# A chain of attention and two feed-forward layers on one core: a broadcast reciprocal row and a shared value product in the first batch

## The chip, the cores and the metric

One core of a Trainium2 chip runs the whole program. The metric is the device time of one execution in microseconds (us). The engines are TensorE (PE for its matmuls, PEld for its weight loads), VectorE (DVE), ScalarE (ACT), GpSimd (POOL) and SyncE (SP), which here only issues DMAs.

## What is computed

The inputs are q, k, v of shape (4, 8, 576, 64) and a decay f of shape (4, 8, 576). The reference, cut to what matters:

```
scores = q k^T / 8 + cum[i] - cum[j]        # cum: running sum of log(clip(f)), causal
attn   = exp(scores - max) / (sum + 1e-9)
x      = attn v                             # then heads side by side: 2304 tokens x 512
h      = x w_in;   g = max(h,0) + alpha*min(h,0);   x = g w_out      # layer 1, 512 -> 2048 -> 512
h      = x w2_in;  g = 0 | (h+1)^2/4 | h;           out = g w2_out   # layer 2
```

The weights of the two layers come as 64-bit floating point.

## The kernel before

The program is written as tasks (`add`: engine, estimated duration, position, dependencies), and `Order.emit` places them into one fixed order per engine, with estimated durations and latencies. An engine then runs its list strictly in that order: an instruction that waits holds up all that stand behind it. Only the order comes from the estimates.

Three kinds of work are laid over one another. The attention runs by units: each of the four batches is cut into a unit of 256 queries and one of 320, and a unit works through four pairs of heads. The conversion (`convert`, 32 pieces of layer 1's weights, w_in and w_out in turn) loads 512 KB, does two passes on ScalarE (L1170, L1203) and five on VectorE (L1173, L1182, L1190, L1195, L1209). Layer 1 (`l1_slice`) goes by chunks of 256 tokens and 16 slices: 12 matmuls L1257, the activation (L1267, L1270, L1276, L1279) and 12 matmuls L1296. The conversion of the first pieces and the first batch's attention start together; later batches and layer 1 share TensorE up to some 550 us, and layer 2 follows.

The first batch (units 0 and 1) takes another way than the later ones, and only it is touched (`plain_pair`). For a pair it loads k, q and v by SP (`load_tok`, L457 and L462), transposes k and q (L558, L576; copies L564, L584), and then goes by groups of two tiles of 64 queries, two heads beside one another on the 128 partitions. Per tile: scores (L622, L624, L627), the minimum on VectorE (`low`, L637), the exponential on ScalarE with the row sum (`expo`, L656), which is in `st`. Per group: the reciprocal of the sums (`rec`, L679 and L680), the multiplication of the whole probabilities by it (`scale`, L686, one VectorE instruction per tile, as wide as the keys: 320 to 576 in unit 1), transposes on TensorE (L704), copies to SBUF (L709), and the value product (L717). In unit 1 there are five tiles, so the third group has one tile alone. A value product has the keys in blocks of 128 and two matmuls to a block, one per head; the stationary operand is a window of `vF` that holds one head's values beside 64 columns of zeros, so both heads add into one PSUM tile `ps_o`. For the lone tile that is 5 blocks, 10 matmuls of 64 columns; each fp32 matmul stands as two records in the trace. At the pair's end ScalarE casts `ps_o` to the high part of x (`xhi`, L739) and VectorE makes the low part (`xlo`, L742).

In the later units the normalisation is another: unnormalised output, the sums gathered, inverted, written to DRAM (L1093) and read back as a broadcast row (L1097), and one VectorE multiplication (L1107).

At the start VectorE clears the rows past the sequence's end in its buffers: L449 for k, L451 for the two q buffers (`qr` for even pairs, three blocks from column 256 on; `qr1` for odd pairs). SP's list begins with f, the first k, q, v, three pieces of weights, alpha (2048 single words) and the second pair's q.

Of the kernel before, what the change touches and what calls it, by code (L numbers as in the profile page):

```python
# [9 lines left out]
F32 = mybir.dt.float32  # L10
# [181 lines left out]
def kernel(  # L192
# [98 lines left out]
    def add(eng, dur, fn, pos, *a, **k):  # L291
# [14 lines left out]
        raw=2, qr=1, qr1=1, q=2, k=2, S=7, M=3, r=2, PH=1, PL=1, s=3, o=1, h=2, g=4, gg=LH + 1,  # L306
        sums=2, rec=2, qd0=1, qd1=1, pA=4, pB=3, pt=4, st=3, sw=2, pty=2, raw2=NRAW, val2=NVAL, x2r=1,
# [84 lines left out]
    def open_phase(n):  # L392
        if n == 1:
            ph["x"] = la.enter_context(ExitStack())
            ph["p"] = ph["x"].enter_context(tc.tile_pool(name="ph1", bufs=1))
            ph["qr"] = ph["p"].tile([P, 3, 2, D], F32, name="qr1")
            names = ("vF",)
# [4 lines left out]
        for nm in names:  # L402
            cnt = NKB if n == 1 else 2 if nm == "vF" else NKB - 2
# [3 lines left out]
            (nc.vector if n == 1 else nc.gpsimd).memset(tf[:, :, 1, :], 0.0 if n == 1 or nm == "vL" else 1.0)  # L407
            if nm == "vF" and S % P:
                for x in (0, 2):
                    (nc.vector if n == 1 else nc.gpsimd).memset(t[S % P:, cnt - 1, x, :], 0.0)  # L410
# [39 lines left out]
    for t in (QR[0], ph["qr"]):  # L450
        nc.vector.memset(t[S % P:, 1:], 0.0)  # L451
# [55 lines left out]
    plain_pv = []  # L507
    attn_tasks = []
# [17 lines left out]
    plain_qk = [[], []]  # L526
    plain_tr = []

    def plain_pair(u, pr, pos_of, prev_pv):
# [12 lines left out]
        def load_q():  # L542
            qb.t = ph["qr"] if pr % 2 else QR[0].rearrange("p c j x d -> p (c j x d)")[:, :3 * P].rearrange(
                "p (c j d) -> p c j d", j=2, d=D)
# [33 lines left out]
        a = last["qtr"] = add("PE", 112 * np_, qtr, p0 - 1, [lq, last.get("qtr")], new=[pb], use=[qb])  # L578
        qready = []
# [10 lines left out]
        def choose():  # L590
# [5 lines left out]
        lv = add("SP", tok_issue(0, nk), lambda: load_tok(V["vF"][:, :, 0:3:2, :], v, b, pr, 0, nk), p0, prev_pv,  # L596
                 move=moved(2 * nk, 256))
# [7 lines left out]
        pvs = []  # L605
        st_new = [st]
        for g in range(-(-nt // 2)):
            tiles = [t for t in (2 * g, 2 * g + 1) if t < nt]
            pg = pos_of(2 * pr + 4 * g / nt)
            ps, sums_ = [], []  # L610
            for t in tiles:
# [57 lines left out]
                pd = []  # L669
                if nkey % P:  # L670
# [3 lines left out]
                    pd = [add("POOL", 150, pad, pg, ex, use=[pbuf])]  # L674
# [7 lines left out]
            rc = add("DVE", 140, rec, pg, sums_, use=[st])  # L682
            pready = []
            for t, (pbuf, nkey, pd) in zip(tiles, ps):
# [4 lines left out]
                pready += [add("DVE", dve2(nkey, True), scale, pg, [rc], use=[pbuf, st])] + pd  # L689
            nb_ = -(-(i0 + tiles[-1] + 1) // 2)  # L690
            per = 4 // len(tiles)
            for kb0 in range(0, nb_, per):
# [18 lines left out]
                def pv(tt=tt, kbs=kbs, nl=nl, w=w, g=g, nb_=nb_, first_=not pvs):  # L711
                    if first_:
                        ob.t = ps_a.tile([P, 512], F32, tag="o0", name="ps_o")
                    tv = tt.t[:, :w].rearrange("p (c t j q) -> p c t j q", t=nl, j=2, q=D)
                    for x, kb_ in enumerate(kbs):
                        for j in range(2):
                            nc.tensor.matmul(  # L717
                                out=ob.t[:, g * P:g * P + nl * D],
                                lhsT=V["vF"][:, kb_].rearrange("p a d -> p (a d)")[:, j * D:j * D + P],
# [7 lines left out]
                a = last["ppv"] = add("PE", 2 * len(kbs) * pe4(P), pv, pg, [a, lv, last.get("ppv")], new=[] if pvs else [ob],  # L727
# [3 lines left out]
        pn = pos_of(2 * pr + 1)  # L731
        t_ = b * S + q0
        o = 0
        while o < n:
# [3 lines left out]
            def xhi(c=c, x0=x0, o=o, m=m):  # L738
                nc.scalar.copy(out=xt(c)[pr][0][:, x0:x0 + m], in_=ob.t[:, o:o + m])  # L739

            def xlo(c=c, x0=x0, o=o, m=m):
                nc.vector.tensor_tensor(out=xt(c)[pr][1][:, x0:x0 + m], in0=ob.t[:, o:o + m],  # L742
                                        in1=xt(c)[pr][0][:, x0:x0 + m].bitcast(F32), op=ALU.subtract)

            a = add("ACT", act(m), xhi, pn, pvs + [("x", c)], use=[ob])
            l = add("DVE", dve(m), xlo, pn, [a], use=[ob])
            X_ready.setdefault(c, []).extend([a, l])
            attn_tasks.extend([a, l])
            o += m
        return pvs  # L750

    for u, pr in head_list():
# [18 lines left out]
        if u == 2 and pr == 0:  # L771
            phase2 = add("X", 0, lambda: open_phase(2), -50, plain_pv + [a for x in plain_qk for a in x])
# [1183 lines left out]
```

## Time and profile before

| what | value |
|---|---|
| median of 3 runs | 1033.4 us (1033.15 to 1033.97) |
| profiled execution, own time | 1034.34 us |
| its span in the trace | 1032.2 us |
| busy PE | 1009.0 us, 98% |
| busy DVE | 793.2 us, 77% |
| busy ACT | 647.5 us, 63% |
| chain that ended last | PE 67%, DVE 20%, ACT 6%, issue 4% |

The share of busy time is a mean over stages; a change to the first 135 us is read from that stretch. A busy TensorE can hide a small wait, since the ends of its matmuls are modelled. The profiled execution's time is 0.94 us over the median.

### The profile page before, as it was taken

To read this page: it belongs to the slowest core of one execution; us is meant where nothing else is said; L and a number is where in the kernel's file an instruction comes from. 1 tells how busy PE (TensorE), PEld (TensorE's weight loads), DVE (VectorE), ACT (ScalarE), POOL (GpSimd) and SP (SyncE) were. 2 spreads that over 40 slices of the span, in tenths; PEclk is the share of its full clock that TensorE was granted. 3 is DMA by queue.
4 is the path that set the end of the run, shared out by engine and by line. 5 is a ranking of instruction groups with operands and counts; after the bars stand their busy time and mean duration, and the time that the engine had idled before them with its cause. 6 is when DMAs were issued, how large, how long until landed. Compare 5 with 4: busy or idle time off the path is not lost.

```text
span 1032.2 us, 19470 instructions
## 1 busy us (share of the span) xinstructions
PE 1009.0 (98%) x6515; PEld 928.7 (90%) x6515; DVE 793.2 (77%) x1956; ACT 647.5 (63%) x1675; POOL 108.8 (11%) x214
## 2 busy tenths in 40 slices
PE   6899999999999999999999999999999999999998
PEld 5789899999999999999999888888889999889886
DVE  7999987878778787787747999987878657655552
ACT  6787789788988888888745655655554334333332
POOL 1000033222322222312100000000000000000000
PEclk9999999999999999999999999999999999999999
DMA  8855024122141212321105667667747544454311
GB/s 234 226 160 180 17 74 95 35 49 60 42 97 37 50 46 46 70 62 38 29 8 178 196 185 231 176 219 252 260 149 254 144 127 121 118 179 119 111 51 62
DMA packets 152482, 123.49 MB, mean 120 GB/s; under 512 B 90144, under 2 KB 122912, under 8 KB 152384
## 3 DMA queue, kind: packets, MB, share of 16 engines
q1 hardware_dynamic: 152384, 122.26, 41.4%
q8 instruction: 52, 0.85, 0.3%
q14 instruction: 46, 0.38, 0.1%
HBM read 93.80 MB, written 28.37 MB: 118 GB/s over the span
## 4 chain that ended last, share of the span: by engine, by line
PE 67%; DVE 20%; ACT 6%; issue 4%; DMA 2%; POOL 1%; SPq 0%; POOLq 0%; ACTq 0%; DVEq 0%
PE ps_z L1535 19%; PE ps_h L1791 11%; PE ps_y L1296 11%; PE ps_h L1257 10%; PE ps_h L1550 6%; PE ps_s L920 3%; DVE w L1209 2%; DVE raw L1190 2%; DVE val L1173 1%; DVE val L1182 1%; DVE raw L1195 1%; DMA raw<-in_moe_w_out_dram 1%; DVE val L1190 1%; DVE val L1195 1%; PE ps_o L1040 1%
## 5 line engine op out<-in xcount | busy, mean ns | idle before, releaser
L1296 PE MATMUL ps_y<-gg,w 128*128 128x256 f32 x1344 | 183.6, 286 | 0.2 <-DVE w L1209 0.2
L1257 PE MATMUL ps_h<-x,w 128*128 128x256 f32 x1344 | 182.6, 285 | 0.1
L1257 PEld LDWEIGHTS ps_h<-x,w 128*128 128x128 f32 x1344 | 169.0, 190 | 1.4 <-issue 0.9
L1296 PEld LDWEIGHTS ps_y<-gg,w 128*128 128x128 f32 x1344 | 168.7, 190 | 1.0 <-DVE w L1209 0.4
L1535 PE MATMUL ps_z<-w,gw 128*128 128x512 f32 x576 | 149.4, 393 | 0.0
L1791 PE MATMUL ps_h<-xc,wc 128*128 128x384 f32 x672 | 136.6, 338 | 0.0
L1791 PEld LDWEIGHTS ps_h<-xc,wc 128*128 128x128 f32 x672 | 121.1, 188 | 10.3
L1535 PEld LDWEIGHTS ps_z<-w,gw 128*128 128x128 f32 x576 | 106.7, 188 | 15.5
L1829 ACT ACTIVATE t<-t,half 128x384 f32<-128x384 f32 x64 | 39.5, 617 | 70.1 <-DVE t L1826 69.7
L1838 ACT CAST gw<-t 128x384 fp32r<-128x384 f32 x64 | 32.8, 512 | 78.8 <-PE ps_z L1535 76.0
L934 ACT ACTIVATE S<-ps_s,nb 128x320 f32<-128x320 f32 (+4 forms) x168 | 75.3, 451 | 9.4 <-PE ps_s L920 8.4
L920 PE MATMUL ps_s<-q,kT 128*128 128x320 f32 (+4 forms) x336 | 72.7, 299 | 3.0 <-DVE kT L833 1.7
L1270 DVE SCALAR_TENSOR_TENSOR g<-g,calpha,ps_h 128x256 f32<-128x256 f32 x112 | 52.7, 475 | 26.5 <-ACT g L1267 25.6
L1535 PE MATMUL ps_z<-w,gg 128*128 128x512 f32 x288 | 72.4, 391 | 0.0
L1841 DVE TENSOR_TENSOR gw<-t,gw 128x384 fp32r<-128x384 f32 x64 | 35.5, 555 | 41.3 <-ACT gw L1838 41.0
L521 POOL TENSOR_SCALAR_AFFINE_SELECT S<-S 128x128 f32<-128x128 f32 (+1 forms) x120 | 42.1, 352 | 237.9 <-ACT S L934 235.3
L1000 ACT ACTIVATE S<-S 128x320 f32<-128x320 f32 (+2 forms) x144 | 60.1, 425 | 6.5 <-DVE S L995 5.9
L979 POOL PARTITION_ALL_REDUCE pp<-pp x48 | 57.3, 1193 | 46.8 <-ACT pp L963 21.5
L1535 PEld LDWEIGHTS ps_z<-w,gg 128*128 128x128 f32 x288 | 53.0, 188 | 9.5
L1279 DVE TENSOR_TENSOR gg<-g,gg 128x256 fp32r<-128x256 f32 x112 | 48.3, 434 | 16.6 <-ACT gg L1276 15.7
L1267 ACT ACTIVATE g<-ps_h 128x256 f32<-128x256 f32 x112 | 42.9, 384 | 28.7 <-PE ps_h L1257 26.7
L995 DVE TENSOR_TENSOR S<-pp,S 128x320 f32<-128x320 f32 (+4 forms) x168 | 57.8, 395 | 2.4 <-POOL pp L979 2.2
(173 smaller groups left out, 2006.5 us busy)
## 6 DMA issues: line engine op xcount, KB each, us to landing
wc<-wc SPq DMA_DIRECT2D x112, 256.0 KB, 2.7
raw<-in_moe_w_in_dram SPq DMA_DIRECT2D x32, 512.0 KB, 4.4
raw<-in_moe_w_out_dram SPq DMA_DIRECT2D x32, 512.0 KB, 5.9
wc<-sh SPq DMA_DIRECT2D x32, 256.0 KB, 2.8
wc<-w SPq DMA_DIRECT2D x24, 256.0 KB, 6.3
out_dram<-osb SPq DMA_DIRECT2D x18, 256.0 KB, 2.5
qr<-in_q_dram SPq DMA_DIRECT2D x64, 64.0 KB, 2.0
raw<-in_k_dram SPq DMA_DIRECT2D x32, 128.0 KB, 2.9
```

What stands on the lines that cost most here:

```text
L920: nc.tensor.matmul(out=sb.t[:, :m], lhsT=kt.t[:, kb * P:(kb + 1) * P], rhs=qt[t].t[:, qo:qo + m], start=(t == 0), stop=(t == 1))
L934: nc.scalar.activation(out=Sb.t[:, so:so + m], in_=sb.t[:, :m], func=AF.Identity, bias=bias)
L979: nc.gpsimd.partition_all_reduce(Mb.t[:, :n], Mx.t[:, :n], P, ReduceOp.max)
L995: nc.vector.tensor_tensor(out=sl, in0=Mb.t[:, qo:qo + m], in1=sl, op=ALU.subtract)
L1000: nc.scalar.activation(out=Sb.t[:, :gn], in_=Sb.t[:, :gn], func=AF.Exp, scale=-SCALE)
L1257: nc.tensor.matmul(out=hb.t, lhsT=a[:, sl], rhs=b, start=(cc == 0 and t == 0), stop=(cc == NCC - 1 and t == 2))
L1270: nc.vector.scalar_tensor_tensor(out=gb.t, in0=gb.t, scalar=calpha[:, s:s + 1], in1=hb.t, op0=ALU.mult, op1=ALU.add)
L1279: nc.vector.tensor_tensor(out=gg.t[1], in0=gb.t, in1=gg.t[0].bitcast(F32), op=ALU.subtract)
L1296: nc.tensor.matmul(out=Y[c][e // 2][:, e % 2, :], lhsT=a[:, sl], rhs=b, start=(s == 0 and t == 0 and e % 2 == 0), stop=(s == NF - 1 and t ...
L1535: nc.tensor.matmul(out=zb.t, lhsT=a, rhs=b, start=(start and t == 0), stop=(stop and t == 2))
L1550: nc.tensor.matmul(out=hb.t, lhsT=a[:, sl], rhs=b, start=(cc == 0 and t == 0), stop=(cc == NCC - 1 and t == 2))
L1791: nc.tensor.matmul(out=hb.t[:, :m], lhsT=wb.t[:, z, sl], rhs=xb.t[y][:, cc, :], start=(begin and cc == 0 and t == 0), stop=(cc == 1 and t ...
```

## The change

In unit 1, pairs 0 to 2 no longer scale their probabilities: the transposes wait for the exponentials alone. When the five tiles' sums are there, `rec` inverts them in one go (128 x 5), SP writes them to DRAM (`put`: 128 runs of 20 bytes) and reads them back (`get`: two DMAs of 64 x 320) into `row`; a filler task of 5000 ns between the two makes the order place the read later. ScalarE takes the whole output to SBUF (`take`), VectorE multiplies it by the row (`norm`, whose row is read with a step of five words), and x is made from there. Unit 0 and pair 3 of unit 1 scale as before (`own`), but pair 3 too goes through `take`.

The lone tile's value product uses one window with both heads' values: 5 matmuls of 128 columns for 10 of 64. The wanted halves then lie at the other head's partitions, and `take` moves them with two copies of 64 x 64. `vF` is laid out anew for it, and its load takes four DMAs instead of three where a half block is left.

The ring of transposed probabilities shrinks from 4 to 3 (its memory holds the taken output). `qr1` is gone: both q buffers are halves of the one tile `qr`, which is cleared whole (64 x 768), and unit 2's first q load waits for all transposes of the first batch's q.

```diff
@@ open_phase
-            ph["qr"] = ph["p"].tile([P, 3, 2, D], F32, name="qr1")
-            names = ("vF",)
+            ph["row"] = ph["p"].tile([P, NMAX], F32, name="row")
+            t = V["vF"] = ph["p"].tile([P, 3 * NKB + 1, D], F32, name="vF", bufs=1)
+            nc.vector.memset(t[:, 0::3, :], 0.0)
+            if S % P:
+                nc.vector.memset(t[S % P:, 3 * NKB - 2:3 * NKB, :], 0.0)
+            return
...
-    for t in (QR[0], ph["qr"]):
-        nc.vector.memset(t[S % P:, 1:], 0.0)
+    nc.vector.memset(QR[0][S % P:], 0.0)
+    QP = [QR[0].rearrange("p c j x d -> p (c j x d)")[:, x * 3 * P:(x + 1) * 3 * P].rearrange(
+        "p (c j d) -> p c j d", j=2, d=D) for x in range(2)]
...
@@ plain_pair
+        def v_at(x):
+            return V["vF"].rearrange("p a d -> p (a d)")[:, x * D:x * D + P]
+
+        def load_v():
+            nf, r = divmod(nk, P)
+            for j in range(2):
+                src = v[b, 2 * pr + j]
+                nc.sync.dma_start(out=V["vF"][:, 2 - j:3 * nf:3, :], in_=src[:nf * P, :].rearrange("(c p) d -> p c d", p=P))
+                if r:
+                    nc.sync.dma_start(out=V["vF"][:r, 3 * nf + 2 - j, :], in_=src[nf * P:nk, :])
...
+        own = u == 0 or pr == NPAIR - 1
...
-            rc = add("DVE", 140, rec, pg, sums_, use=[st])
-            pready = []
-            for t, (pbuf, nkey, pd) in zip(tiles, ps):
+            pready = [x for _, _, pd in ps for x in pd]
+            rc = add("DVE", 140, rec, pg, sums_[2 * g:], use=[st]) if own else None
+            for t, (pbuf, nkey, pd) in zip(tiles, ps) if own else ():
...
+                    if nl == 1:
+                        for x, kb_ in enumerate(kbs):
+                            nc.tensor.matmul(
+                                out=ob.t[:, g * P:g * P + P], lhsT=v_at(3 * kb_ + 1), rhs=tt.t[:, x * P:(x + 1) * P],
+                                start=first_ and x == 0, stop=kb_ == nb_ - 1, skip_group_check=True)
+                        return
...
+        def put():
+            nc.sync.dma_start(out=spread.rearrange("j (q t) -> (j q) t", t=nt), in_=stats()[:, 2, :nt])
+
+        def get():
+            db.t = ph["row"]
+            for j in range(2):
+                nc.sync.dma_start(out=db.t[j * D:(j + 1) * D, :n], in_=spread[j:j + 1, :].to_broadcast([D, n]))
+
+        def take():
+            rb.t = SS[:, 3 * 512 + rb.slot * NMAX:3 * 512 + (rb.slot + 1) * NMAX]
+            m = n // P * P
+            nc.scalar.copy(out=rb.t[:, :m], in_=ob.t[:, :m])
+            if m < n:
+                for j in range(2):
+                    hr = slice(j * D, (j + 1) * D)
+                    nc.scalar.copy(out=rb.t[hr, m:n], in_=ob.t[D - j * D:2 * D - j * D, m + j * D:m + (j + 1) * D])
+
+        def norm():
+            o_ = rb.t[:, :n].rearrange("p (t q) -> p t q", q=D)
+            nc.vector.tensor_tensor(out=o_, in0=o_, in1=db.t[:, :n].rearrange("p (q t) -> p t q", t=nt), op=ALU.mult)
+
+        src = ob
+        ml = pvs
+        if u:
+            e = add("ACT", act(n) + (300 if n % P else 0), take, pn, pvs, new=[rb], use=[ob])
+            src, ml = rb, [e]
+        if not own:
+            a = add("DVE", 330, rec, pn, sums_, use=[st])
+            a = add("SP", 400, put, pn, [a], use=[st], move=moved(P, 4 * nt))
+            a = add(f"wait{pr}", 5000, lambda: None, pn, [a])
+            a = add("SP", 1350, get, pn, [a], new=[db], move=moved(P, 4 * n))
+            ml = [add("DVE", dve(n), norm, pn, [a, e], use=[rb, db])]
...
-        last["lq"] = add("SP", tok_issue(q0, q1), load_q, p0 - 3, [last.get("lq")], new=[qb_], move=moved(2 * n, 256))
+        last["lq"] = add("SP", tok_issue(q0, q1), load_q, p0 - 3, [last.get("lq")] + plain_qtr * (u == 2),
+                         new=[qb_], move=moved(2 * n, 256))
```

Three places show how the order moves. In the rows, DVE_49 and PE_49 are the counters that VectorE and TensorE raise, DMAHW0 to DMAHW7 those of landed DMAs; a count is not printed. First, SP's list at the program's start, before:

```order
L473 DMA raw_166<-in_f_dram 32x576
L457 DMA raw_167<-in_k_dram 128x2x64 x2
L457 DMA qr<-in_q_dram 128x2x64 x2
L457 DMA vF<-in_v_dram 128x2x64 x2
L1156 DMA raw<-in_moe_w_in_dram 128x4x128
L1156 DMA raw<-in_moe_w_out_dram 128x512 [waits DMAHW0_49]
L1156 DMA raw<-in_moe_w_in_dram 128x4x128 [waits DMAHW1_49]
L1158 DMA alpha_sb<-in_moe_alpha_dram 128x16x1 [waits DMAHW2_49]
```

and now:

```order
L478 DMA raw_165<-in_f_dram 32x576
L462 DMA raw_166<-in_k_dram 128x2x64 x2
L462 DMA qr<-in_q_dram 128x2x64 [waits DVE_49]
L462 DMA qr<-in_q_dram 128x2x64
L611 DMA vF<-in_v_dram 128x2x64 x2
L1224 DMA raw<-in_moe_w_in_dram 128x4x128
L1224 DMA raw<-in_moe_w_out_dram 128x512 [waits DMAHW0_49]
L1224 DMA raw<-in_moe_w_in_dram 128x4x128 [waits DMAHW1_49]
L1226 DMA alpha_sb<-in_moe_alpha_dram 128x16x1 [waits DMAHW2_49]
```

The first q load, which waited for nothing, now waits for VectorE: it writes rows and columns that the clearing of the whole `qr` (now L454) also writes.

Second, VectorE's list at the end of unit 1's pair 0 (L679, L680 and L699, L700 are a group's reciprocal, L762, L763 the pair's). Before:

```order
L663 TENSOR_TENSOR st<-st 128x1
L1190 SCALAR_TENSOR_TENSOR raw<-raw,val 128x512
L679 TENSOR_SCALAR st<-st 128x1
L680 RECIPROCAL st<-st 128x1
L1195 SCALAR_TENSOR_TENSOR raw<-raw 128x512
L686 TENSOR_SCALAR pp<-pp,st 128x576
```

and now, with the rows from the pair's reciprocal, 21 left out, to its multiplication by the row:

```order
L683 TENSOR_TENSOR st<-st 128x1
L1258 SCALAR_TENSOR_TENSOR raw<-raw,val 128x512
L762 TENSOR_SCALAR st<-st 128x5
L763 RECIPROCAL st<-st 128x5
...
L1277 TENSOR_TENSOR w<-raw,w 128x512
L1258 SCALAR_TENSOR_TENSOR raw<-raw,val 128x512
L784 TENSOR_TENSOR S<-S,row 128x320
```

The scalings are gone, the three reciprocals are one, and the multiplication stands 21 instructions behind it. In pair 1 it is also 21 behind, in pair 2 it is 29.

Third, SP's list around pair 0's write and read of the reciprocals, which is new:

```order
L766 DMA spread_0_175<-st 128x5 [waits DMAHW7_49,DVE_49]
L1224 DMA raw<-in_moe_w_out_dram 128x512 [waits DMAHW0_49]
L1224 DMA raw<-in_moe_w_in_dram 128x4x128 [waits DMAHW1_49]
L611 DMA vF<-in_v_dram 128x4x64 [waits DMAHW2_49,PE_49]
L613 DMA vF<-in_v_dram 64x64 [waits DMAHW3_49,PE_49]
L611 DMA vF<-in_v_dram 128x4x64 [waits DMAHW4_49]
L613 DMA vF<-in_v_dram 64x64 [waits DMAHW5_49]
L771 DMA row<-spread_0_175 64x320 [waits DMAHW7_49,DMAHW6_49]
L771 DMA row<-spread_0_175 64x320
```

Between the write and the read stand two loads of weights and the next pair's v, which waits for TensorE's value product of the pair.

## Rows read from the trace of the kernel before

**Rows 1.** The page's first part: busy time, share, instructions.

```profile
PE 1009.0 (98%) x6515; PEld 928.7 (90%) x6515; DVE 793.2 (77%) x1956; ACT 647.5 (63%) x1675; POOL 108.8 (11%) x214
```

**Rows 2.** Busy time by stretch: length, PE, PEld, DVE, ACT, POOL, clock, DMA, GB/s.

```profile
0.00:14.00 14.00, 6.53 (x26) 5.26 (x26) 9.70 (x34) 7.14 (x15) 3.75 (x16) 1.00 0.68 169
14.00:40.00 26.00, 22.73 (x139) 19.64 (x137) 23.39 (x73) 21.16 (x65) 2.53 (x13) 1.00 0.88 241
40.00:56.00 16.00, 14.40 (x101) 12.34 (x102) 15.86 (x41) 11.13 (x27) 0.79 (x2) 1.00 0.87 236
56.00:110.00 54.00, 54.00 (x405) 48.83 (x404) 53.51 (x132) 41.00 (x102) 2.23 (x8) 1.00 0.48 152
110.00:160.00 50.00, 47.94 (x375) 44.32 (x373) 46.14 (x119) 39.20 (x114) 11.06 (x24) 1.00 0.23 57
```

**Rows 3.** Timeline of SP at the start: start us, us, instruction, count.

```profile
2.16 0.98 SPq L457 DMA_DIRECT2D qr<-in_q_dram  x2
...
4.21 0.47 SPq L1156 DMA_DIRECT2D raw<-in_moe_w_in_dram  x1
...
5.74 0.51 SPq L1158 DMA_DIRECT2D alpha_sb<-in_moe_alpha_dram  x1
6.36 5.08 SPq L457 DMA_DIRECT2D qr<-in_q_dram  x2
```

**Rows 4.** Timeline of DVE and ACT at the start; landings of the weights' loads (L1156).

```profile
5.28 0.76 DVE L451 MEMSET qr<- 64x512 f32 x2
...
9.28 1.22 ACT L1170 ACTIVATE val<-raw 128x512 f32<-128x512 f32 x2
...
10.42 0.42 DVE L1173 TENSOR_SCALAR val<-val 128x512 f32<-128x512 f32 x1
...
DMA to landing us min/median/max: 4.9/6.6/7.0
```

**Rows 5.** Timeline of PE, end of unit 1's pair 0.

```profile
61.34 1.16 PE L717 MATMUL ps_o<-S,vF 128*128 128x128 f32 x8
62.33 0.27 PE L704 MATMUL pst<-ident,pp 128*128 128x128 f32 x1
...
63.29 1.98 PE L717 MATMUL ps_o<-S,vF 128*128 128x64 f32 x16
65.11 0.97 PE L622 MATMUL ps_s<-kT,qd 128*128 128x448 f32 x2
...
66.15 0.63 PE L717 MATMUL ps_o<-S,vF 128*128 128x64 f32 x4
66.62 0.65 PE L622 MATMUL ps_s<-kT,qd 128*128 128x512 f32 x1
```

**Rows 6.** Timeline of DVE: reciprocals (L679, with L680) and scalings (L686) of unit 1.

```profile
60.01 0.52 DVE L686 TENSOR_SCALAR pp<-pp,st 128x576 f32<-128x576 f32 x1
...
65.24 0.16 DVE L679 TENSOR_SCALAR st<-st 128x2 f32<-128x2 f32 x1
...
65.51 0.67 DVE L1195 SCALAR_TENSOR_TENSOR raw<-raw 128x512 int32<-128x512 int32 x1
66.10 0.71 DVE L686 TENSOR_SCALAR pp<-pp,st 128x320 f32<-128x320 f32 x2
66.72 0.62 DVE L637 TENSOR_REDUCE st<-ps_s 128x1 f32<-128x448 f32 x1
...
72.60 0.84 DVE L686 TENSOR_SCALAR pp<-pp,st 128x448 f32<-128x448 f32 x2
73.35 0.69 DVE L1209 TENSOR_TENSOR w<-raw,w 128x512 fp32r<-128x512 f32 x1
```

**Rows 7.** Later units' normalisation: the multiplication (ns min/median/max); the row's read (us to landing).

```profile
L1107 DVE TENSOR_TENSOR pp<-pp x12: 410/482/941, 159.5 to 521.0; 128x256 f32<-128x256 f32 x6, 128x320 f32<-128x320 f32 x6
...
m<-spread SPq DMA_DIRECT2D x12, 80.0 KB, 2.8
```

**Rows 8.** Groups by form, 0 to 130 us: ScalarE's cast of the output.

```profile
L739 ACT CAST x<-ps_o 128x256 fp32r<-128x256 f32 x7 | 2.6, 371 | 0.0
```

More of the change, by code (lines that the diff above doesn't have):

```diff
@@ L526 @@
     plain_qk = [[], []]
+    plain_qtr = []
     plain_tr = []
@@ L668, in plain_pair @@
                     sums_ += ex
-                pd = []
+                pd = list(ex)
                 if nkey % P:
@@ L672, in pad @@
                         nc.gpsimd.memset(pbuf.t[:, nkey:nkey + D], 0.0)
-                    pd = [add("POOL", 150, pad, pg, ex, use=[pbuf])]
+                    pd.append(add("POOL", 150, pad, pg, ex, use=[pbuf]))
                 ps.append((pbuf, nkey, pd))
@@ L687, in scale @@
                                             scalar2=None, op0=ALU.mult)
[L689 removed]
+                pready.append(add("DVE", dve2(nkey, True), scale, pg, [rc], use=[pbuf, st]))
             nb_ = -(-(i0 + tiles[-1] + 1) // 2)
@@ L726, in plain_pair @@
                 a = add("ACT", act(w), pcopy, pg, [a], new=[tt], use=[tb])
-                a = last["ppv"] = add("PE", 2 * len(kbs) * pe4(P), pv, pg, [a, lv, last.get("ppv")], new=[] if pvs else [ob],
+                a = last["ppv"] = add("PE", (1 if len(tiles) == 1 else 2) * len(kbs) * pe4(P), pv, pg, [a, lv, last.get("ppv")], new=[] if pvs else [ob],
                                       use=[tt, ob] if pvs else [tt])
@@ L731, in plain_pair, with rec @@
         pn = pos_of(2 * pr + 1)
+        rb, db = Buf(R["rb"]), Buf(R["row"])
+        spread = tc.dram_tile([2, D * nt], F32, name=f"spread{u}_{pr}")
+        def rec():
+            nc.vector.tensor_scalar(out=stats()[:, 2, :nt], in0=stats()[:, 1, :nt], scalar1=1e-9, scalar2=None, op0=ALU.add)
+            nc.vector.reciprocal(out=stats()[:, 2, :nt], in_=stats()[:, 2, :nt])
+        def put():
[26 more added lines that the diff above has]
+            ml = [add("DVE", dve(n), norm, pn, [a, e], use=[rb, db])]
+        plain_end.extend(ml)
         t_ = b * S + q0
@@ L771 @@
         if u == 2 and pr == 0:
-            phase2 = add("X", 0, lambda: open_phase(2), -50, plain_pv + [a for x in plain_qk for a in x])
-            for nm, users in (("S", plain_pv), ("M", plain_tr), ("r", plain_tr), ("sums", plain_tr)):
+            phase2 = add("X", 0, lambda: open_phase(2), -50, plain_end + plain_pv + [a for x in plain_qk for a in x])
+            for nm, users in (("S", plain_pv + plain_x), ("M", plain_tr), ("r", plain_tr), ("sums", plain_tr)):
                 for x in range(len(R[nm].slots)):
```

33 lines of the change are left out of this document (18 added, 15 removed).

## The prediction

> **What bounds the kernel now.** I read the share of busy time first [rows 1]: TensorE is busy for 1009.0 of the 1032.2 us span, so it stands idle for 23.2 us, and a change that takes no work from TensorE can give back no more than that. Next the table by stretch [rows 2] tells where: 7.5 us of idle TensorE lie in the first 14 us, 3.3 us up to 40, 1.6 us up to 56, none from 56 to 110, 2.1 us up to 160, and the remaining 8.8 us lie later, where nothing is touched. The same rows show the particular state of the first batch: from 40 to 110 us VectorE is busy for 69.4 of 70 us, TensorE for 68.4. Both are full. Taking work from one alone would leave the other in charge; this change takes from both. Behind 160 us TensorE has work waiting, so whatever delay or lead it has there is carried to the end. The account is therefore TensorE's: its work, plus its idle time. I then read SP's timeline at the start, since the order shows a new wait there.
>
> **Removed on TensorE.** In pair 0 the lone tile's 10 matmuls are 20 records: 16 run from 63.29 to the next matmul at 65.11, four from 66.15 to 66.62, together 2.29 us [rows 5]. The five that replace them are 10 records of 128 columns. Eight such records take from 61.34 to 62.33, 0.124 us each, so ten take 1.24 us. That saves 1.05 us a pair, and four pairs **4.2 us**, on an engine that is full.
>
> **Removed on VectorE.** A pair's five scalings are 0.62 us (66.10 to 66.72), 0.75 us (72.60 to 73.35) and 0.52 us, in all 1.89. A reciprocal with its addition holds VectorE for 0.27 us (65.24 to 65.51) [rows 6], and two of three go: 0.54. The new multiplication costs 0.48 us by the same shape of the later units [rows 7]. Net 1.95 us a pair, **5.9 us** for three. Its row is read with a step of five words, which no row shows; between 0.48 us and twice that, I take 0.48, because no other difference is to be seen, and keep the 1.4 us for three pairs.
>
> **Added at the start.** The first q load goes out at 2.16 us now [rows 3]. It will wait until the q buffers are cleared, which ends at 5.28 + 0.76 = 6.04 us [rows 4]; the cleared area is the same, so that end hardly moves. SP's list is in order, so all behind it moves by 3.9 us: v, the weights (4.21 to 8.1), alpha, and the second pair's q, which is held up for 5.08 us behind alpha now and will be there too. ScalarE starts on the first weights at 9.28, 5.07 us after their issue; by the landings (4.9 at the least, 6.6 in the middle) [rows 4] it will start between 13.0 and 14.7. I take 13.2, the old distance, since the same loads follow one another. VectorE's first conversion step, now at 10.42, follows ScalarE's 0.6 us pass at about 13.8: **3.4 us** later, 3.2 to 4.9 as bounds. Before and after, VectorE's first row minimum stands behind two such steps, and the exponentials behind the minimum. So the conversion being late stalls the attention too, and I see nothing that catches up: from 14 to 40 us VectorE is busy for 23.4 of 26 us and DMA for 0.88 of the time [rows 2].
>
> **Costed at nothing.** ScalarE's `take` is three copies a pair, none wider than the cast of 0.37 us [rows 8], at most 4.5 us for four pairs; ScalarE has 13 us free from 56 to 110 [rows 2]. Without that cover x would come later, and x is needed first by layer 1's second chunk, after chunk 0's sixteen slices. SP's write, two reads and one more v load add some 2 us a pair to a queue that mostly waits; the two weight loads behind the write are late by the wait for the sums, and the conversion loads up to seven pieces ahead. Unit 2's q load waits for transposes that precede unit 1's last scores anyway. The ring of three instead of four can hold a copy up; I leave that to the range.
>
> **The sum.** TensorE: +3.4 at the start, -4.2 of work. VectorE: +3.4, -5.9. VectorE comes out 1.7 us further ahead than TensorE, and TensorE's idle time in 40 to 56 and 110 to 160 us, 3.7 us in all [rows 2], can shrink, by nothing at least and by 3.7 at most. I credit **0.8 us**, near the lower end, because half of it lies behind 110 us, where the order is laid out anew, and because the multiplication may wait for its row. In all 3.4 - 4.2 - 0.8 = -1.6 us. Against the profiled execution's 1034.34 that is 1032.7; this execution stands 0.94 over the median, so against the median of 1033.4 it is **1031.8 us**. That is -0.15%. About 0.2%, 2.1 us, is what a measurement of this kernel can tell from no change, so my likeliest case ends as no change, close to the edge.
>
> **Rivals.**
> (a) *The late loads are covered.* VectorE and ScalarE are idle for 4.3 and 6.9 us in the first 14 us [rows 2], and if the order there had room, the 3.4 us would vanish: -5.0, 1028.4 us. Against it: a list in order does not use room behind a wait. The wait not being where I think, on the clearing, would give the same. Chance 0.15.
> (b) *TensorE's idle time goes altogether*, as its transposes no longer wait for a scaling: 3.4 - 4.2 - 3.7 = -4.5, 1028.9 us. For it: VectorE is full in just these 16 us from 40 to 56. Against it: 2.1 of the 3.7 us come after the scalings. Chance 0.13.
> (c) *The multiplication waits for its row* and VectorE, which runs in order, stands with it. This is the side of slower. The read stands behind the next pair's v, and v waits for the pair's last product. In pair 0 now the lone tile's scaling starts at 60.01 [rows 6] and its product ends at 66.62 [rows 5]; without the 0.5 us of scaling that is 6.1 us from the sums, and with up to 1.9 us for four v issues (0.47 each by the load at 4.21 [rows 3]), 0.5 for the second read's issue and 2.8 to land [rows 3, 7], the row is there 11.3 us after the sums. The multiplication stands 21 instructions behind, 8.5 us by the stretch's mean of 53.5 us for 132 [rows 2], some 10 since most of the 21 are conversion steps of about 0.6. So a wait of 1 to 3 us is possible if TensorE's product comes no earlier than now. With w us a pair VectorE's account is 3.4 - 5.9 + 3w, and it passes TensorE's -0.8 from w = 0.6 on, and +2.1 from w = 1.5 on; at 2 us it is +3.5, 1036.9 us. Against it: the new order puts the lone tile's product sooner, with no scaling ahead of it, and the order reckons with the read's landing. Chance 0.17.
> (d) *Nothing of TensorE's idle time goes*, since VectorE's lead is spent: 3.4 - 4.2 = -0.8, 1032.6 us. The row's read with a step of five words would do it: at twice 0.48 us for three pairs VectorE's lead over TensorE falls from 1.7 to 0.3 us. Chance 0.15. The Trainium skill has a rule that speaks for this: SBUF — State Buffer, section "Door 1", says that SBUF is read in lines of 16 bytes and that each access which goes to a new line pays; a step of five words goes to a new line with every element. It gives no price, and no row here shows such a read on VectorE.
>
> **How the numbers follow.** The forecast keeps 0.40, with a range of its own of 1030.4 to 1033.2 (the credit of 0.8 moved by 1.4 either way). About 0.12 of that lies below 1031.3, the bound of faster. Faster: 0.15 + 0.13 + 0.12 = 0.40. Same: 0.28 + 0.15 = 0.43. Slower: 0.17. The range reaches down to (a) and (b), and up so far that only the upper half of (c), and a later landing at the start, are left out: 1028.2 to 1036.0.
>
> **What would show it.** Right: SP's first q load at about 6.1 us instead of 2.16, ScalarE's first conversion pass near 13.2, VectorE's near 13.8 with some 3.4 us of idle time put down to that pass; ten records for each lone tile in about 1.24 us; no scalings but in pair 3 after unit 0; the multiplication at about 0.48 us with no DMA named as its releaser; TensorE full again from about 59 us. Wrong: the first unit catching up before 56 us, idle VectorE ahead of the multiplication, more than 3 us of idle TensorE between 110 and 160 us, or a difference that arises behind 200 us.

## The result, and the profile after

The changed kernel takes 1039.28 us (median of 4 runs, 1038.71 to 1040.0) against 1033.6 us of the kernel before beside it: ratio 1.0055, 95% interval 1.0038 to 1.0073. It is slower by 5.7 us, where 1031.8 us was forecast, with 1036.0 as the upper end. Below, a ratio is turned into us on 1033.5 us; all are against the kernel before on the same chip. The medians give up to 0.7 us otherwise, and the recorded expectations went by them (-2.4 us for s5, where its ratio gives -2.8). A difference between two of the kernels, each with its own interval, is uncertain by 1.3 to 2.0 us.

The first part of the page and the busy time by stretch, to be laid beside [rows 1] and [rows 2] (the same columns):

```profile
span 1037.9 us, 19347 instructions
PE 1005.7 (97%) x6475; PEld 928.8 (89%) x6475; DVE 790.1 (76%) x1930; ACT 649.8 (63%) x1687; POOL 111.0 (11%) x214
```

```profile
0.00:14.00 14.00, 5.41 (x22) 4.39 (x23) 6.93 (x24) 4.32 (x7) 3.74 (x16) 1.00 0.47 140
14.00:40.00 26.00, 20.82 (x128) 18.68 (x127) 22.99 (x72) 20.98 (x62) 1.99 (x10) 1.00 0.83 217
40.00:56.00 16.00, 15.04 (x100) 12.35 (x99) 15.62 (x36) 12.79 (x34) 0.68 (x3) 1.00 0.98 254
56.00:110.00 54.00, 53.83 (x395) 47.85 (x395) 52.48 (x126) 45.33 (x117) 2.51 (x12) 1.00 0.60 176
110.00:160.00 50.00, 42.81 (x311) 40.82 (x310) 46.93 (x116) 40.08 (x114) 13.19 (x23) 0.90 0.21 55
```

The span is 5.7 us longer, though TensorE is busy for 3.3 us less. So 9.0 us of idle time have come: 2.6 us up to 110 us, and 5.1 us between 110 and 160 (7.19 for 2.06), where the granted clock also fell to 0.90. Behind 160 us some 1.3 us are added.

**The start** went as its rows said. Timelines of SP, VectorE and ScalarE, beside [rows 3] and [rows 4]:

```profile
6.10 0.88 SPq L462 DMA_DIRECT2D qr<-in_q_dram  x2
...
8.04 0.47 SPq L1224 DMA_DIRECT2D raw<-in_moe_w_in_dram  x1
```

```profile
5.37 0.70 DVE L454 MEMSET qr<- 64x768 f32 x1
...
13.47 0.43 DVE L1241 TENSOR_SCALAR val<-val 128x512 f32<-128x512 f32 x1 [1.44 <-ACT val L1238]
```

```profile
12.77 0.67 ACT L1238 ACTIVATE val<-raw 128x512 f32<-128x512 f32 x1 [1.87 <-DMA raw<-in_moe_w_in_dram]
```

The first q load moved from 2.16 to 6.10 us, the first weights from 4.21 to 8.04, and VectorE's first conversion step from 10.42 to 13.47. ScalarE's first pass starts 4.73 us after the weights' issue (12.77, last row).

**The lone product and the multiplication.** Timeline of TensorE at pair 0 (the five matmuls are L736, ten records), and VectorE's group by form of the multiplication by the row (L784):

```profile
63.48 1.05 PE L736 MATMUL ps_o<-S,vF 128*128 128x128 f32 x8
64.37 0.27 PE L724 MATMUL pst<-ident,pp 128*128 128x128 f32 x1
...
65.47 0.47 PE L736 MATMUL ps_o<-S,vF 128*128 128x128 f32 x2
65.78 0.60 PE L724 MATMUL pst<-ident,pp 128*128 128x128 f32 x4
```

```profile
L784 DVE TENSOR_TENSOR S<-S,row 128x320 f32<-128x320 f32 x3 | 2.2, 750 | 0.0
```

The product takes 0.89 + 0.31 = 1.20 us for 2.29 [rows 5]. The multiplication takes 0.75 us for 0.48 [rows 7], with no idle time ahead of it.

**Between 110 and 160 us.** What TensorE waited for there, one line per wait (us in total, times, longest):

```profile
PE ps_s L988 <- DVE kT L901: 3.9, 2, 2.4
PE ps_h L1325 <- DVE g L1338: 1.5, 1, 1.5
PE ps_s L988 <- DVE q L925: 1.3, 1, 1.3
```

L988 makes the scores of unit 2, the second batch's first. VectorE's timeline at the first two of these waits, and TensorE's:

```profile
131.80 0.42 DVE L901 TENSOR_TENSOR kT<-pst,kT 64x256 fp32r<-64x256 f32 x1
132.25 0.69 DVE L1277 TENSOR_TENSOR w<-raw,w 128x512 fp32r<-128x512 f32 x1
132.86 1.10 DVE L1258 SCALAR_TENSOR_TENSOR raw<-raw,val 128x512 int32<-128x512 int32 x1
134.00 0.43 DVE L901 TENSOR_TENSOR kT<-pst,kT 64x256 fp32r<-64x256 f32 x1
134.45 0.69 DVE L1263 SCALAR_TENSOR_TENSOR raw<-raw 128x512 int32<-128x512 int32 x1
135.06 0.62 DVE L1063 TENSOR_TENSOR S<-pp,S 128x256 f32<-128x256 f32 x2
135.71 0.43 DVE L925 TENSOR_TENSOR q<-pst,q 128x256 fp32r<-128x256 f32 x1
```

```profile
131.78 0.39 PE L1102 MATMUL ps_o<-S,vF 128*128 128x128 f32 x2
134.57 0.35 PE L988 MATMUL ps_s<-q,kT 128*128 128x256 f32 x1 [2.40 <-DVE kT L901]
136.19 0.90 PE L988 MATMUL ps_s<-q,kT 128*128 128x256 f32 x3 [1.27 <-DVE q L925]
...
138.55 2.91 PE L1325 MATMUL ps_h<-x,w 128*128 128x256 f32 x12
141.26 0.63 PE L988 MATMUL ps_s<-q,kT 128*128 128x256 f32 x2
```

VectorE is busy for 4.17 of the 4.30 us from 131.80 to 136.10. The k and q passes that TensorE wants (L901, L925) stand in its list between steps of the conversion (L1258, L1263, L1277), and TensorE, in order too, stands behind the scores. Unit 2's first scores, in the kernel before and here:

```profile
130.02 0.47 PE L920 MATMUL ps_s<-q,kT 128*128 128x256 f32 x2
```

```profile
117.24 0.51 PE L988 MATMUL ps_s<-q,kT 128*128 128x256 f32 x2
```

They come 12.8 us sooner now, because the list has changed: before, 13 slices of layer 1 and 28 conversions stood ahead of unit 2's first scores and first k pass; now it is 9 and 23.

### The profile page after: what moved, and what is told of

The parts are those of the page before. It is cut to its first block, busy times and chain, and to the rows that moved or that the text cites. A ratio compares the mean times of both kernels' runs of the same rounds, so it can differ in the third digit from the quotient of the medians.

```text
span 1037.9 us, 19347 instructions
## 1 busy us (share of the span) xinstructions
PE 1005.7 (97%) x6475; PEld 928.8 (89%) x6475; DVE 790.1 (76%) x1930; ACT 649.8 (63%) x1687; POOL 111.0 (11%) x214
## 4 chain that ended last, share of the span: by engine, by line
PE 81%; DVE 9%; ACT 5%; issue 2%; DMA 1%; POOL 1%; SPq 0%; ACTq 0%; POOLq 0%; DVEq 0%
PE ps_z L1603 19%; PE ps_y L1364 12%; PE ps_h L1859 11%; PE ps_h L1325 11%; PE ps_h L1618 6%; PE ps_y L1452 4%; PE ps_h L1408 4%; PE ps_s L988 3%; PE ps_s L642 1%; PE ps_o L1102 1%; PE ps_o L1108 1%; PE ps_o L1110 1%; PE ps_o L1109 1%; DVE S L1063 1%; PE ps_o L743 1%
## 5 line engine op out<-in xcount | busy, mean ns | idle before, releaser
L1859 PEld LDWEIGHTS ps_h<-xc,wc 128*128 128x128 f32 x672 | 121.1, 188 | 10.3
L988 PE MATMUL ps_s<-q,kT 128*128 128x320 f32 (+4 forms) x336 | 73.0, 300 | 8.4 <-DVE kT L901 6.2
L528 POOL TENSOR_SCALAR_AFFINE_SELECT S<-S 128x128 f32<-128x128 f32 (+1 forms) x120 | 44.4, 373 | 253.2 <-ACT S L1002 247.6
L988 PEld LDWEIGHTS ps_s<-q,kT 128*128 128x128 f32 x336 | 54.3, 193 | 10.3 <-PE ps_o L1102 2.6
```

The lines of the kernel that those rows point to most:

```text
L528: nc.gpsimd.affine_select(out=sl, in_=sl, pattern=[[1, sl.shape[1]]], compare_op=ALU.is_ge, fill=NEG, base=base, channel_multiplier=-1)
L988: nc.tensor.matmul(out=sb.t[:, :m], lhsT=kt.t[:, kb * P:(kb + 1) * P], rhs=qt[t].t[:, qo:qo + m], start=(t == 0), stop=(t == 1))
L1859: nc.tensor.matmul(out=hb.t[:, :m], lhsT=wb.t[:, z, sl], rhs=xb.t[y][:, cc, :], start=(begin and cc == 0 and t == 0), stop=(cc == 1 and t ...
```

## The experiments

Two theories stood against one another. A: the new order is the cause of the stall, the late start a price of its own. B: the order is harmless, and the stall is there because the conversions come 3 us late. Four kernels take the parts apart.

**s1_start**, the changed kernel with a small clearing, so that q need not wait; every list is otherwise the same:

```diff
-    nc.vector.memset(QR[0][S % P:], 0.0)
+    for x in range(2):
+        nc.vector.memset(QR[0].rearrange("p c j x d -> p (c j x d)")[S % P:, (3 * x + 2) * P:(3 * x + 3) * P], 0.0)
```

> The changed kernel, but the q buffer is cleared only where no first load writes (two blocks of 128 columns instead of all 768), so that the first q load need not wait; the order of all other work is the changed one. Theory A (order): in the changed kernel's order the second batch's first scores stand four layer-1 slices sooner and their VectorE passes fall among the last nine conversions; this alone makes TensorE idle between 110 and 160 us. Then SP's first q load is back at about 2.2 us, all shifts 3 us to the left, and the time falls by about 3.0 to some 1036.3 us; TensorE's idle time from about 107 to 157 us stays at 6 to 7 us. Theory B (start): the stall is only there because the conversions are 3 us late. Then the time falls by 3 and by the 5 us of that stall, to 1031 us or below, and the idle time of that stretch is 2 to 3 us.

Measured: ratio 1.0015 (1.0006 to 1.0024), +1.6 us. The late start cost 4.1 us here. The stall stays, in busy time by stretch:

```profile
110.00:160.00 50.00, 42.82 (x312) 41.01 (x312) 46.75 (x116) 40.13 (x116) 14.33 (x24) 0.90 0.21 53
220.00:500.00 280.00, 274.63 (x2230) 271.76 (x2230) 215.80 (x595) 232.74 (x686) 69.80 (x120) 1.00 0.23 52
```

**s2_before_late**, the kernel before with the whole clearing:

```diff
-    for t in (QR[0], ph["qr"]):
-        nc.vector.memset(t[S % P:, 1:], 0.0)
+    nc.vector.memset(QR[0][S % P:], 0.0)
+    nc.vector.memset(ph["qr"][S % P:, 1:], 0.0)
```

> The kernel before with one thing of the change: all of the q buffer is cleared, so that the first q load waits; its order is the one before. Theory A (order): the price is the late start alone, 3.0 to 3.4 us, 1036.4 to 1036.8 us, with TensorE's idle time from 110 to 160 us near the 2.1 of before. Theory B (start): the late conversions also bring the stall, so 1040 us or more, with some 7 us of idle TensorE from 110 to 160 us. Neither: the delay is made up somewhere, and the time is within 1 us of before.

Measured: 1.0032 (1.0019 to 1.0044), +3.3 us, and no stall:

```profile
110.00:160.00 50.00, 47.93 (x369) 44.01 (x368) 46.32 (x119) 38.97 (x110) 9.70 (x22) 1.00 0.20 50
```

B has fallen: a late start alone brings no stall, and without a late start the stall is there.

**s3_lone** (every pair scales as before) and **s4_row** (the lone product for each head apart), both with the small clearing, in this order:

```diff
-        own = u == 0 or pr == NPAIR - 1
+        own = True
```

```diff
-                    if nl == 1:
+                    if False:
...
-            m = n // P * P
+            m = n
...
-                a = last["ppv"] = add("PE", (1 if len(tiles) == 1 else 2) * len(kbs) * pe4(P), pv, pg, [a, lv, last.get("ppv")], new=[] if pvs else [ob],
+                a = last["ppv"] = add("PE", 2 * len(kbs) * pe4(P), pv, pg, [a, lv, last.get("ppv")], new=[] if pvs else [ob],
```

> The changed kernel with the small clearing, and every pair normalised as before by scaling its weights; what is left of the change is the lone query block's shared value product. Its order has the second batch's first scores at the 12th slice (14th before, 10th in the changed kernel), and the first kT pass on VectorE behind 26 conversions (28 before, 23 in the changed kernel). Theory A (order): TensorE's work falls by 4.2 us, and part of it is lost to a smaller stall between 110 and 160 us of 3 to 5 us: 1030 to 1033 us. Theory B (start): no late start, so no stall: 4.2 us less than before, 1029.3 us.

> The changed kernel with the small clearing, but the lone query block's value product made for each head apart, as before; what is left of the change is the normalisation by a row. Its order has the second batch's first scores at the 10th slice and the first kT pass behind 24 conversions, as the changed kernel. Theory A (order): no work is taken from TensorE, and the stall between 110 and 160 us is there with 5 to 7 us: 1037 to 1040 us. Theory B (start): no late start, so no stall: 1033.4 us less up to 3 us of TensorE's idle time, 1030.5 to 1033.5 us.

Measured: both 1.0028 (1.0018 to 1.0038), +2.9 us. Idle TensorE from 110 to 160 us is 5.1 and 4.9 us, at clocks of 0.86 and 0.93. So each part of the change is slower than the kernel before, in its own re-laid order; s3_lone too, though it takes 4.2 us of work from TensorE. (Both keep the changed kernel's `take`, its v loads and its ring of three, so neither is a part quite alone.) B's figures for both were 3 us too low or more. A's figure for s3_lone (1030 to 1033 us) was too low as well, and its figures for s4_row (1037 to 1040 us, 5 to 7 us of idle time) were just too high.

Next, the order itself. The planner places unit 2's first three transposes; a dependency on a conversion holds them back:

```diff
+    for t in held[:3]:
+        t.deps.append(W_ready[1, 27][1])
```

(`held` lists the k and q transposes of later units; 27 is the 28th conversion.) **s5_hold28** is s1_start with this; **s6_floor8** gives unit 2 a later position instead, **s7_conv_first** the conversions an earlier one; **s8_unit_step** reads the row word after word (its queries are multiplied by other queries' reciprocals; only the time of the read is looked at). The first three set A against a third theory, C: VectorE has as much to do as ever before its last conversion, wherever unit 2 stands, so TensorE's idle time only moves and the time stays within 1.5 us of s1_start's. Edits of s6, s7 and s8:

```diff
-            return (x * 24 - 60 if x < 1 else NF + (x - 1) * RATE - LEAD) + off
+            return (x * 24 - 60 if x < 1 else max(NF + (x - 1) * RATE - LEAD, 8)) + off
```

```diff
-    WOFF = -8
+    WOFF = -10
```

```diff
-            nc.vector.tensor_tensor(out=o_, in0=o_, in1=db.t[:, :n].rearrange("p (q t) -> p t q", t=nt), op=ALU.mult)
+            nc.vector.tensor_tensor(out=o_, in0=o_, in1=db.t[:, :n].rearrange("p (t q) -> p t q", t=nt), op=ALU.mult)
```

> The changed kernel with the small clearing, and the second batch's first three transposes on TensorE wait, in the planner's list, for the 28th conversion: its first scores are at the 14th slice and its first kT pass behind 28 conversions, as in the kernel before. Theory A (order): with that place restored TensorE's idle time from 107 to 160 us falls from 7.2 to about 2 us, its clock stays at full speed, and the saved products count: 1029 to 1031 us. Theory C (work): VectorE has as much to do before the last conversion as ever, and TensorE, whose attention is done 14 us sooner, runs dry wherever the second batch stands; the idle time only moves, to the slices that wait for conversions, and the time stays within 1.5 us of the 1035.2 with the small clearing alone.

> The changed kernel with the small clearing, and the whole first unit of the second batch gets a position of at least 8 in the planner's list instead of 4, so that conversions (up to 6.5) go first wherever both are ready: first scores at the 14th slice, first kT pass behind 26 conversions, the third kT pair behind all 32. Theory A (order): 1029 to 1031 us with 2 to 3 us of idle TensorE from 107 to 160 us. Theory C (work): within 1.5 us of 1035.2, with idle time ahead of slices that wait for conversions.

> The changed kernel with the small clearing, and the conversions two positions earlier in the planner's list (10 slices ahead instead of 8); the second batch keeps its place: first scores at the 11th slice, first two kT passes behind 24 and 25 conversions, the next behind 30. It changes the other side of the same meeting. Theory A (order): between the changed order and the one before, 1031 to 1034 us. Theory C (work): within 1.5 us of 1035.2.

> The changed kernel with the small clearing, with the row of reciprocals read word after word instead of with a step of five words; the row stays laid out as it was, so that the queries of the three pairs are multiplied by other queries' reciprocals, and only the read's speed is looked at. If the step of the read is what made the multiplication 0.75 us, it takes 0.48 us now, as the later units' of the same shape; if the row's or the product's place in memory made it, 0.75 us stays. The time: 0.3 us less for each of three multiplications at the most, so no more than 0.8 us.

Measured: s5 0.9973 (0.9964 to 0.9983), -2.8 us; s6 1.0000 (0.9991 to 1.0010); s7 0.9985 (0.9975 to 0.9994), -1.6 us. Against s1_start s5 gives 4.3 us back, s7 3.1 and s6 1.6. So the place of unit 2 counts, against C's figure; but the idle time did move, as C said. The hold's 4.3 us are about what A said, but not where A said. In s5 no wait for a k or q pass is left between 110 and 160 us, yet others take their place. The two stretches of s5, then of s6:

```profile
110.00:160.00 50.00, 43.88 (x337) 42.07 (x336) 44.08 (x112) 39.16 (x113) 10.65 (x22) 0.93 0.20 51
220.00:500.00 280.00, 278.27 (x2262) 275.57 (x2260) 218.90 (x599) 235.85 (x689) 70.16 (x120) 1.00 0.23 52
```

```profile
110.00:160.00 50.00, 46.92 (x382) 45.25 (x382) 45.59 (x117) 40.47 (x119) 12.03 (x22) 1.00 0.23 61
220.00:500.00 280.00, 273.76 (x2187) 268.95 (x2186) 215.30 (x594) 234.24 (x685) 70.43 (x120) 0.99 0.23 52
```

s6 nearly removes the stall (3.1 us idle, full clock) and gains less than s5, which keeps 6.1 us of it. From 110 to 220 us the hold brings nothing: 8.0 us of idle time in s5, 7.2 in s1_start. Its gain shows behind 220 us: idle 5.4 us in s1_start, 1.7 in s5, 6.2 in s6. s7 is like s5 in this, with 7.0 us from 110 to 160 and 2.5 behind 220. Idle TensorE in us, from such rows:

| stretch | before | after | s1_start | s5_hold28 | s6_floor8 |
|---|---|---|---|---|---|
| 0 to 110 | 12.3 | 14.9 | 11.1 | 10.3 | 11.1 |
| 110 to 160 | 2.1 | 7.2 | 7.2 | 6.1 | 3.1 |
| 160 to 220 | 1.4 | 0.0 | 0.0 | 1.9 | 1.4 |
| 220 to 500 | 2.8 | 5.2 | 5.4 | 1.7 | 6.2 |
| sum | 18.6 | 27.3 | 23.7 | 20.0 | 21.8 |
| span | 1032.2 | 1037.9 | 1034.4 | 1030.0 | 1032.0 |

With 3.1 to 3.3 us less of busy time in each changed kernel than before, the sums give the differences of the spans to within 0.5 us. The order costs in two places: where the second batch meets the last conversions, and in the later units, whose lists are laid out anew with it. There the same scores wait for the same k pass, as the groups of TensorE from 220 to 500 us show, s1_start first, then s5 (busy us, mean ns, idle time ahead and its releasers):

```profile
L989 PE MATMUL ps_s<-q,kT 128*128 128x320 f32 (+3 forms) x240 | 51.4, 296 | 3.3 <-DVE kT L902 2.5 <-ACT kT L899 0.8
```

```profile
L992 PE MATMUL ps_s<-q,kT 128*128 128x320 f32 (+3 forms) x240 | 51.5, 297 | 0.6 <-DVE kT L904 0.5
```

s8's multiplications took 484 ns each, so the step of five words is what made them 0.75 us. Its one run, 1035.06 us, stands beside s1_start's 1035.18 on another chip: no difference that one run can tell.

```profile
L785 DVE TENSOR_TENSOR S<-S,row 128x320 f32<-128x320 f32 x3 | 1.5, 484 | 0.0
```

Then the hold with the other parts, and other places of it (`W_ready[1, 25]` is s11, `W_ready[1, 29]` s12). **s9_late_hold28** is the changed kernel with the hold alone, **s10_lone_hold28** is s3_lone with it:

> The changed kernel as it is, with its large clearing and late first load, and only the second batch's first three transposes held until the 28th conversion. Against the kernel before, the small clearing alone gave +1.6 us and the same with this hold -2.4 us; the late load cost 3.3 us in the kernel before and 4.1 in the changed one. If start and order are two prices of their own, it is -2.4 + 3.3 to 4.1: 0.9 to 1.7 us over the kernel before. If the late start only hurts where the conversions meet the second batch, the hold takes that price away too: 1 to 2.4 us under the kernel before. If the hold makes TensorE wait for a conversion that is 3 us late, 3 us or more over it.

> The shared value product of the lone block alone (small clearing, every pair normalised by scaling its weights), which came out 2.9 us over the kernel before, with the second batch's first three transposes held until the 28th conversion: first scores at the 15th slice instead of the 12th. Theory A (order): the saved products count now, 2 to 4 us under the kernel before. Rival: it is not the order but VectorE, which has all its scalings here and ends its conversions no sooner; the time stays 2 to 3 us over the kernel before.

> The changed kernel with the small clearing and the hold at the 26th conversion: first scores at the 13th slice, first kT pass behind 27 conversions. With no hold (10th slice) it is 1.6 us over the kernel before, with 28 conversions (14th slice) 2.4 us under it. Theory A (order): in between, from 1 us over to 2.4 us under.

> The changed kernel with the small clearing and the hold at the 30th conversion: first scores at the 16th slice, first kT pass behind 30 conversions. Theory A (order) has a best place: past it TensorE has only slices left, which wait for the last conversions, and the second batch comes late. Then it is slower than with 28 by 1 to 3 us, near the kernel before. If TensorE still finds work there, it is equal to the one with 28 or better, 2.4 to 4 us under the kernel before.

Measured: s9 1.0001 (0.9992 to 1.0009); s10 1.0002 (0.9992 to 1.0011); s11 0.9981 (0.9972 to 0.9990), -2.0 us; s12 1.0038 (1.0024 to 1.0052), +3.9 us. In the changed kernel as it is, one dependency gives 5.6 us back. The late start costs 2.9 us in the held order (s9 against s5), 4.1 in the changed one, 3.3 in the one before: a price of its own, that the hold does not take away, though s9 came out just under the 0.9 to 1.7 us over the kernel before that this theory gave. The hold has a best place: none +1.6, 26th -2.0, 28th -2.8, 30th +3.9 us; the 26th and the 28th are not told apart, and the 30th costs more than the 1 to 3 us expected. s10 gained 2.7 us over s3_lone, not the 5 to 7 that A gave it: it lies between A's figure and its rival's, and with every scaling kept the shared product brings nothing measurable even with the hold.

So even with start and order mended the gain is 2.8 us, where my sum without the late start gives 5.0. The last four kernels take each engine's saving back without moving any instruction of the lists: in s13 and s15 the lone product is made for each head apart (the first two edits of s4_row, not its planned cost), in s14 and s16 VectorE does more behind each new multiplication (rb.t is its output).

```diff
+            for _ in range(6):
+                nc.vector.tensor_scalar(out=rb.t[:, :n], in0=rb.t[:, :n], scalar1=1.0, scalar2=None, op0=ALU.mult)
```

> The changed kernel with the small clearing and exactly its order, but each lone tile's product is made for the two heads apart (20 records instead of 10; ScalarE then takes it over in one copy instead of three): the saving on TensorE is taken back without moving anything. If TensorE's work counts in full, as the sum of the prediction had it, the time rises by 4.2 us over the 1.6 us that the small clearing alone stands above the kernel before, to +5.8 us. If VectorE is what the first 150 us wait for, the saving only became idle time, and taking it back costs 0 to 1.5 us: +1.6 to +3.1 us.

> The changed kernel with the small clearing and exactly its order, with six more multiplications by one of 128x320 words on VectorE behind each of the three new multiplications, some 0.3 us each by the scalings' rows, 5 us in all: about what the change took from VectorE. If TensorE's account is the one that counts, 0 to 1 us more than the small clearing alone: +1.6 to +2.6 us against the kernel before. If VectorE is what is waited for, all of it: +6 to +7 us.

> The same two products for each lone tile, in the order with the hold at the 28th conversion, which alone is 2.4 us under the kernel before. If TensorE's work counts in full in this order: 1.8 us over the kernel before. If VectorE is still what is waited for: 1 to 2.4 us under it.

> The same eighteen multiplications more on VectorE, in the order with the hold at the 28th conversion. If VectorE is what is waited for: some 5 us more than the 2.4 us under the kernel before, +2 to +3 us. If TensorE's account counts there: 1.5 to 2.4 us under it.

Measured: s13 1.0024 (1.0014 to 1.0034), +2.5 us; s14 1.0076 (1.0062 to 1.0090), +7.9 us; s15 0.9992 (0.9983 to 1.0001), -0.8 us; s16 1.0040 (1.0028 to 1.0053), +4.1 us. VectorE's group of the added multiplications in s14 (in s16 they come to the same 6.0 us):

```profile
L787 DVE TENSOR_SCALAR S<-S 128x320 f32<-128x320 f32 x18 | 6.0, 335 | 0.6
```

| worth of | changed order | held order |
|---|---|---|
| 4.2 us of products on TensorE | 0.9 us | 2.0 us |
| 6.0 us more on VectorE | 6.3 us | 6.9 us |

Each entry is uncertain by 1.3 us for TensorE and by 1.7 for VectorE, so the two orders are not told apart. But VectorE's work counts in full, TensorE's by about a quarter to a half, and never by the whole 4.2 us: in these orders the first batch ends on VectorE's account. s13 came out within the bounds for VectorE as the limit; s15 just short of them (1 to 2.4 us under the kernel before), s14 and s16 above theirs (+6 to +7, +2 to +3 us). (In s13 and s15 ScalarE is also spared two short copies a pair, 0.21 us each in the changed kernel; that was not taken apart.)

## Why the prediction was wrong

**What bounds the kernel: the step that failed first.** "The account is therefore TensorE's: its work, plus its idle time." As an identity it holds, as the table of idle time shows. As a sum it failed, because I put the saved 4.2 us in full and let the idle time move on its own by 0.8 at most. The two are tied: up to some 150 us it is VectorE's list, most of it conversions, that lets TensorE go on, and half or more of the work taken from TensorE there became idle time (0.9 and 2.0 us of 4.2 counted, s13 and s15). I had read from [rows 2] that both engines are full from 40 to 110 us; a TensorE that shows as busy was not one whose work sets the pace. This was tried in the changed and the held order, not in the order before.

**The credit for idle time: the step that turned the sign.** I reckoned that TensorE's idle time "can shrink, by nothing at least and by 3.7 at most". It grew by 5.1 us from 110 to 160 us, and by 9.0 us in all. I had set aside the reason myself, "because half of it lies behind 110 us, where the order is laid out anew", and then bounded the term at nothing from below. Nothing excluded a loss. The first scores and k passes of unit 2 in the two lists (the 10th slice for the 14th; behind 23 conversions for 28) were there to be read. Likewise "later, where nothing is touched" was wrong: the planner lays the later units anew, and 220 to 500 us lost 2.4 us.

**The start: right in the wait and its carrying on.** +3.05 us at VectorE's first conversion step for a forecast of 3.4, just below my lower bound of 3.2: the first weights let ScalarE start 4.73 us after their issue, sooner than the 4.9 that I had taken as the least. In time it is 3.3 us when it is put alone into the kernel before (s2). With s1_start the cheap cure is shown: clear only what no early load writes.

**The lone product: right in size, wrong in worth.** 1.20 us for ten records against 1.24 forecast; what it brings is 0.9 to 2.0 us, not 4.2.

**VectorE's saving.** The multiplication took 0.75 us, between my bounds of 0.48 and 0.96, so three pairs save 0.8 us less than the 5.9 I put; the page shows 3.1 us less of busy VectorE in all, and the other 2.0 us were not taken apart. What the saving brings by itself is known only roughly: s15, which has it without the shared product, is 0.8 us under the kernel before, and s10, which lacks it, 3.0 over s5, but in lists of its own. That work added there counts in full is measured (s14, s16); that work taken away there counts in full is not shown, and 0.8 us is far from it.

**The rivals.** None of (a) to (d) happened. (a) and (b) are excluded by s2 and by the idle time. Of (c), my only slower case, nothing is seen: the multiplication has no idle time ahead of it, and VectorE's one wait above 0.3 us from 70 to 112 us is for a weight cast of ScalarE. The slow read that (d) named is there: with a step of five words the multiplication takes 750 ns, with a step of one and nothing else changed 484 ns (s8), 1.55 times. The Trainium skill's page SBUF — State Buffer, section "Door 1", says that each access that goes to a new line of 16 bytes pays. The runs agree. But by (d)'s price of at most 1.4 us the kernel would have been at 1032.6 us; it isn't what made it slow. The slow side came from the order, which I had costed as none.

**The sum, afterwards.** Late start +4.1 (the changed kernel against s1_start), order +4.3 (s1_start against s5), what is left of both savings -2.8 (s5): 5.6 us in all, for 5.7 measured. These are differences of a chain, so that they add up is no proof; that start and order are separate prices is shown by s2 and s9. The 2.2 us that are missing from my 5.0 are about what the products fall short of 4.2 in the held order, where they bring 2.0; with an uncertainty of 1.3 us that is an agreement, no proof.

**Left open.** What the half clock alone costs; the last section has a hint. What the ring of three instead of four places does to the order was not tried; in the changed kernel no copy into it (L729) waited for a place, since its only waits, 3.7 us in four, are for transposes. And how the idle time of s5 could go too: it waits at other places (2.7 us of it for ScalarE's PH at 146 us).

**A version that beats both:** s5_hold28, the change with the small clearing and one dependency, at 0.9973 (0.9964 to 0.9983) of the kernel before.

## What to carry to other kernels

Where a planner sets the order, a change of one stage's work is two changes, and the second, the new list, can be worth more than the first: read in both lists where the next stage's first work stands against the stage that feeds it, and bound that term on both sides. Which of two full engines sets the pace is found by adding a few us of idle work to each at a fixed order; of work taken from the other one, much turns into waiting. A buffer that is cleared whole makes every load into it wait for the clearing, and at the head of an in-order queue that delays all that stands behind.

## What the runs showed of the hardware that I had not expected

TensorE's granted clock halved after a short drought in the middle of the changed kernel, while before it stands at 1.00 in all stretches of [rows 2]. Rows of 1 us in the changed kernel (columns as in [rows 2]):

```profile
131.00:132.00 1.00, 1.00 (x10) 0.97 (x9) 0.97 (x4) 1.00 (x4) 0.00 (x0) 1.00 0.55 124
...
133.00:134.00 1.00, 0.00 (x0) 0.00 (x0) 0.97 (x2) 0.65 (x1) 0.87 (x1) 1.00 0.00 0
134.00:135.00 1.00, 0.35 (x1) 0.19 (x1) 0.97 (x2) 0.00 (x0) 0.00 (x0) 1.00 0.00 0
135.00:136.00 1.00, 0.00 (x0) 0.00 (x0) 0.97 (x4) 0.82 (x2) 0.00 (x0) 0.65 0.00 0
...
140.00:141.00 1.00, 1.00 (x6) 1.00 (x6) 1.00 (x3) 1.00 (x5) 0.32 (x1) 0.50 0.08 6
```

Between 132.2 and 136.2 us only one matmul of 0.35 us ran; then the clock is at 0.50, its lower level of 1.2 GHz. Twelve matmuls of 128x256 take 2.71 us there (138.55 to 141.26, above) and 1.48 us at full speed:

```profile
143.50 1.65 PE L1364 MATMUL ps_y<-gg,w 128*128 128x256 f32 x12
144.98 0.28 PE L1108 MATMUL ps_o<-PH,vH 128*128 128x256 f32 x1
```

So a wait of 3.7 us for VectorE (2.40 + 1.27) goes on to cost at the next matmuls. How much of the 5.7 us that is can't be read from the sums of busy time: s13, with the products of before, is busy for 1009.6 us against 1009.0, though its clock from 110 to 160 us is 0.90. One kernel's own executions give a hint: six of s1_start's eleven show a mean clock of 0.993 or 0.994 and take 1035.9 us in the mean, five show 0.997 or 0.998 and take 1034.6. That is 1.3 us with the same order. Whether the lower clock made them longer or longer waits the clock lower is not shown.
